# A fused attention and FFN kernel: statistics of the layer norms ahead of the FFN on VectorE, and the first four output groups of each expansion on token halves

## The chip, the cores and the metric

The kernel runs on one core of a Trainium2 chip. The metric is device time of one execution in microseconds (us); the number that counts is the median of several runs. The core has engines that work side by side, each through its own queue in order: TensorE (PE in the profile, its weight loads PEld), VectorE (DVE), ScalarE (ACT), GpSimd (POOL) and SyncE (SP), which here issues all large DMA transfers.

## What is computed

Two layers, each an attention block and a feed-forward block with residuals, on 2048 tokens of width 1024, in bfloat16:

```python
def _layernorm(x, axis=-1, eps=1e-5):
    m = jnp.mean(x, axis=axis, keepdims=True)
    v = jnp.var(x, axis=axis, keepdims=True)
    return (x - m) / jnp.sqrt(v + eps)
...
def _A_ref(x, wqkv, wo):     # 32 heads of 32; 8 keys per token, 2 tokens apart
    ...
    logits = jnp.einsum("bhsd,bhswd->bhsw", q, kg) * scale
    logits = jnp.where(mask[None, None, :, :], logits, -1e9)
    attn = _softmax(logits, axis=-1)
    o = jnp.einsum("bhsw,bhswd->bhsd", attn, vg)
    ...
def _B_ref(x, w1, b1, w2, b2):   # 1024 -> 3584 -> 1024
    h = jnp.einsum("bsd,df->bsf", x, w1) + b1
    r = jnp.where(h > zero, h, zero)
    h = r * r
    return jnp.einsum("bsf,fd->bsd", h, w2) + b2
...
x = x + _A_ref(_layernorm(x), A_wqkv, A_wo)
x = x + _B_ref(_layernorm(x), B_w1, B_b1, B_w2, B_b2)
x = x + _A_ref(_layernorm(x), A_wqkv, A_wo)
x = x + _B_ref(_layernorm(x), B_w1, B_b1, B_w2, B_b2)
```

## The kernel before

The tokens are cut into four blocks of 512 (even and odd tokens are kept apart, so that keys two tokens apart are neighbours). A layer and a block make a unit: units 0 to 3 are layer one, 4 to 7 layer two. A unit goes through six stages, each a Python generator:

- `gen_SA`: loads four tiles of 128 tokens, normalises each (`ln_transpose`) and transposes it by DMA into `xnT`, features on partitions. This is the attention norm.
- `gen_SQ` in two parts, `SQa` (K and Q) and `SQb` (V): L260 multiplies weights with `xnT`, ScalarE copies the result out of PSUM (L262).
- `gen_S2`: the windowed attention, on VectorE. L308 multiplies Q with shifted K, L327 adds the products in a tree, TensorE reduces over the head (L354, 16 small matmuls of 32 columns for each half of 256 tokens; L341 in unit 0), then softmax (L364 to L378), a DMA transpose of the probabilities (`pb`, L388), and the product with V (L401 to L404) into `oT`.
- `gen_SW`: the output projection (L447), residual `xm` (L449, VectorE), the FFN norm (`ln_transpose` of `xm` into a second `xnT`), and L453, which adds the bias b2 to `xm` once the norm has read it.
- `gen_SF`: the FFN, in two halves of the 3584 features (16 and 12 groups of 128). A group is a chain of eight L475 matmuls, 512 tokens wide, into the PSUM tile `ph`; ScalarE makes `r` (L479, bias and ReLU) and `r2t` (L480, square). L496 multiplies the squares of a half with w2.

`ln_transpose` has two ways to the statistics. With `dve_stats` two `bn_stats` (L171) and one `bn_aggr` (L173) on VectorE give mean and variance; ScalarE takes the logarithm and the exponential for the reciprocal root (L175, L176), and VectorE multiplies to `nmr` (L177). Without it ScalarE does all: a pass for the sum (L180), a scaling (L182), a pass for the squares (L184), logarithm, exponential and `nmr` (L186 to L188). Both passes are written into the tile `xn`. In both cases L189 on ScalarE writes the normalised tile to `xn` (two buffers) and L190 transposes it (SP queue, SyncE waits for `xn`, the DMA takes some us). Before the change VectorE takes the statistics in `gen_SA` of unit 0 and in `gen_SW` of unit 7, ScalarE in all others.

`build` writes the order of the program. The primary stages stand in the row SQa(0), SQb(0), then for each u: SQa(u+1), SW(u), SQb(u+1), SF(u). At each `yield` of a primary stage a position is counted up and `service` moves the side tasks (SA, S2) on by their launch and due positions: S2(u+1) runs beside SW(u), SQb(u+1) and SF(u), SA(u+2) beside SF(u). This written order is a priority for a scheduler, which places each engine's instructions by estimated readiness; what is under `high_priority` (L262, L449, L479, L480 and the sums of L502 to L511) goes first. The order on each engine is fixed when the program is built. Waits between engines are put in by the tile framework from reads and writes of tiles, for the part of a tile that is read.

PSUM has six tiles for `py`, `pq` and `ph` together (`ps_mm`) and two for the attention logits. Weights come in tiles of 1 MB through five buffers, issued by SP three ahead of use (`get_w`). `xnT` has two buffers, `xt` two.

Of the kernel before, what the change touches and what calls it, by code (L numbers as in the profile page):

```python
# [7 lines left out]
F32 = mybir.dt.float32  # L8
# [9 lines left out]
BLK = 512  # L18
# [8 lines left out]
class _Kernel:  # L27
# [403 lines left out]
    def gen_SW(self, u):  # L431
        nc = self.nc
        layer, b = divmod(u, self.NB)
        KD, KF, NCH, D, F = self.KD, self.KF, self.NCH, self.D, self.F
        st = self.state[u]
        oT = st.pop("oT")
        xnT = self.act.tile([128, KD, BLK], BF, name="xnT", tag="xnT")
        wos = [self.get_w(("wo", u, g)) for g in range(D // 512)]
        xbs = []
        for tl in range(4):  # L440
            t = b * 4 + tl
            xr = self.load_x_tile(layer, t, "xt")
            xm = self.xp.tile([128, D], F32, name="xm", tag="xm", bufs=4)
            for db in range(D // 512):
                py = self.ps_mm.tile([128, BLK], F32, name="py", tag="mm")
                for c in range(NCH):
                    nc.tensor.matmul(py[:], oT[:, c, tl * 128:(tl + 1) * 128], wos[db][:, c, :], start=(c == 0), stop=(c == NCH - 1))  # L447
                with self.tc.high_priority():
                    nc.vector.tensor_tensor(xm[:, db * 512:(db + 1) * 512], py[:], xr[:, db * 512:(db + 1) * 512], ALU.add)  # L449
                yield  # L450
            xbs.append(xm)
            self.ln_transpose(xm[:], xnT, tl, dve_stats=(u == self.n_layers * self.NB - 1), evac_act=(u == 0))
            nc.vector.tensor_tensor(xm[:], xm[:], self.b2b[:], ALU.add)  # L453
            yield
        st["xnT_B"] = xnT
        st["xbs"] = xbs

    def gen_SF(self, u):
        nc = self.nc
        layer, b = divmod(u, self.NB)  # L460
        KD, KF, NCH, D, F = self.KD, self.KF, self.NCH, self.D, self.F
        st = self.state[u]
        xnT = st.pop("xnT_B")
        xbs = st.pop("xbs")
        last_layer = (layer == self.n_layers - 1)
        NHALF = len(self.f_halves)
        for hf, (g0, g1) in enumerate(self.f_halves):
            r2 = []
            for g in range(g0, g1):
                wt = self.get_w(("w1", u, g))  # L470
                for cc in range(4):
                    f_idx = g * 4 + cc
                    ph = self.ps_mm.tile([128, BLK], F32, name="ph", tag="mm")
                    for kd in range(KD):
                        nc.tensor.matmul(ph[:], wt[:, kd, cc * 128:(cc + 1) * 128], xnT[:, kd, :], start=(kd == 0), stop=(kd == KD - 1))  # L475
                    r = self.small.tile([128, BLK], BF, name="r", tag="r", bufs=3)
                    r2t = self.r2p.tile([128, BLK], BF, name="r2t", tag="r2")
                    with self.tc.high_priority():
                        nc.scalar.activation(out=r[:], in_=ph[:], func=ACTF.Relu, bias=self.b1T[:, f_idx:f_idx + 1], scale=1.0)  # L479
                        nc.scalar.activation(out=r2t[:], in_=r[:], func=ACTF.Square)  # L480
                    r2.append(r2t)
                    yield
            final = (hf == NHALF - 1)
            KFH = 4 * (g1 - g0)
            for db in range(D // 512):
                w2s = [self.get_w(("w2", u, hf, db, gi)) for gi in range(len(self.w2_groups[hf]))]
                kmap = []
                for gi, (k0, k1) in enumerate(self.w2_groups[hf]):
                    for j in range(k1 - k0):
                        kmap.append((gi, j))  # L490
                for tl in range(4):
                    t = b * 4 + tl
                    py = self.ps_mm.tile([128, BLK], F32, name="py2", tag="mm")
                    for kf in range(KFH):
                        gi, j = kmap[kf]
                        nc.tensor.matmul(py[:], r2[kf][:, tl * 128:(tl + 1) * 128], w2s[gi][:, j, :], start=(kf == 0), stop=(kf == KFH - 1))  # L496
                        if kf % 7 == 6 and kf != KFH - 1:
                            yield
                    xbsl = xbs[tl][:, db * 512:(db + 1) * 512]
                    if not final:  # L500
                        with self.tc.high_priority():
                            nc.vector.tensor_tensor(xbsl, py[:], xbsl, ALU.add)  # L502
                    elif last_layer:
                        xo = self.small.tile([128, BLK], BF, name="xo", tag="xo", bufs=3)
                        with self.tc.high_priority():
                            nc.vector.tensor_tensor(xo[:], py[:], xbsl, ALU.add)  # L506
                        nc.sync.dma_start(self.par_tile(self.out_par, t)[:, db * 512:(db + 1) * 512], xo[:])
                    else:
                        xo = self.small.tile([128, BLK], F32, name="xof", tag="xof", bufs=2)
                        with self.tc.high_priority():  # L510
                            nc.vector.tensor_tensor(xo[:], py[:], xbsl, ALU.add)  # L511
                        nc.sync.dma_start(self.xs[layer][t * 128:(t + 1) * 128, db * 512:(db + 1) * 512], xo[:])
                    yield

        st["sf_done"] = True
# [15 lines left out]
    def build(self):  # L531
# [33 lines left out]
        def advance(t, upto):  # L565
            if t['gen'] is None:
                t['gen'] = gens[t['kind']](t['u'])
            while not t['finished'] and t['done'] < upto:
                try:
                    r = next(t['gen'])  # L570
                    if r == "BLOCK":
                        assert upto < t['n'] + 500, "blocked generator at forced completion"
                        break
                    t['done'] += 1
                except StopIteration:
                    t['finished'] = True

        def service(pos):
            for t in tasks:
                if t['finished'] or pos < t['launch']:  # L580
                    continue
                span = max(1, t['deadline'] - t['launch'])
                f = (pos - t['launch']) / (span * t['margin'])
                tgt = t['n'] + 1 if (f >= 1.0 or pos >= t['deadline']) else f * t['n']
                advance(t, tgt)

        pos = 0
        for i, (kind, u) in enumerate(prim):
            for t in tasks:
                if not t['finished'] and t['deadline'] <= cum[i]:  # L590
                    advance(t, t['n'] + 1000)
            g = gens[kind](u)
            for _ in g:
                pos += 1
                service(pos)
            pos = cum[i + 1]
            service(pos)
# [52 lines left out]
```

## Time and profile before

| what | value |
|---|---|
| median of 3 runs | 1322.74 us (1322.34 to 1323.29) |
| span of the profiled execution, first to last instruction | 1317.7 us |
| granted TensorE clock, mean | 0.988 |
| TensorE busy | 94% of the span |
| VectorE, ScalarE busy | 62%, 48% |
| DMA, mean | 189 GB/s |
| L475 matmuls, 128x512 (1792) | 383 ns each, by the record |
| L260 matmuls, 128x512 (1536) | 381 ns each, by the record |
| L479, L480 on ScalarE (224 each) | 682 ns, 627 ns |
| L180, L184, L189 on ScalarE, from `xm` (28, 28, 32) | 1054, 1148, 1241 ns |
| L308, L327 on VectorE (128, 98) | 1224, 1218 ns |
| transposes of `xn` (64), issue to landing | 3.5 us median |

The time of the profiled execution is given by its span alone; the runs' times hold start and end besides. Matmuls overlap, so a record is longer than the distance from one start to the next (0.216 us for 512 columns where nothing waits); on VectorE and ScalarE neighbours overlap by about 0.1 us in the records. Groups are told by line, engine, operation and names; after the bar stand busy time, mean of one, and the idle time before them with what ended it.

### The profile page before, as it was taken

The page shows a single profiled execution, that of the slowest core. Times are in us where ns is not written, and L with a number is a line of the kernel's source. Part 1 is how long each engine was busy: PE and PEld are TensorE (multiplying, and loading weights), DVE is VectorE, ACT ScalarE, POOL GpSimd, SP SyncE. Part 2 cuts the span into 40 slices and gives each one's busy share as a digit, 9 for nine tenths or more (in the row PEclk, how much of TensorE's full clock was granted, in tenths as well). Part 3 has the DMA queues.
Part 4 walks back from the last instruction along what each step waited for, and adds up shares of the span by engine and source line. Part 5 has one row for each costly group of instructions (what it writes and reads, how often), then busy time and mean ns, then how long its engine had stood idle before and what let it go on. Part 6 is the DMA issues. An engine that isn't in the chain of part 4 may idle for free.

```text
span 1317.7 us, 15544 instructions
## 1 busy us (share of the span) xinstructions
PE 1243.7 (94%) x6112; PEld 633.7 (48%) x6112; DVE 811.7 (62%) x1132; ACT 636.8 (48%) x1185; POOL 2.9 (0%) x9
## 2 busy tenths in 40 slices
PE   2998899998999999999999999999999999996998
PEld 1664444554445544465444654455544554442443
DVE  2569997197932969239781597617794199915011
ACT  3633854159342682427912396314944167142622
POOL 0000000000000000000000000000000000000000
PEclk9998899999999999999999999999999999998999
DMA  9573883668747695558955589455984578448341
GB/s 247 153 199 97 220 217 123 214 194 230 176 144 239 191 241 169 165 194 231 250 172 186 199 234 245 160 192 176 260 235 132 195 219 221 134 150 227 128 136 56
DMA packets 282218, 248.77 MB, mean 189 GB/s; under 512 B 109984, under 2 KB 245152, under 8 KB 282144
## 3 DMA queue, kind: packets, MB, share of 16 engines
q1 hardware_dynamic: 278544, 247.76, 64.0%
q0 software_dynamic: 3600, 0.01, 0.5%
q8 instruction: 48, 0.79, 0.2%
q14 instruction: 26, 0.21, 0.1%
HBM read 209.98 MB, written 12.58 MB: 169 GB/s over the span
## 4 chain that ended last, share of the span: by engine, by line
PE 63%; ACT 18%; DVE 9%; DMA 8%; issue 2%; SPq 0%; ACTq 0%; DVEq 0%
PE py L496 28%; PE ph L475 19%; PE pq L260 13%; DMA xnT<-xn 5%; DVE P L308 3%; ACT r L479 3%; ACT xn L180 3%; ACT xn L189 3%; ACT xn L184 3%; ACT r2t L480 3%; DVE P L327 2%; PE py L447 2%; DMA xt<-xs 1%; ACT vT L262 1%; DMA xt<-in_A_x_dram 1%
## 5 line engine op out<-in xcount | busy, mean ns | idle before, releaser
L475 PE MATMUL ph<-xnT,wt 128*128 128x512 bf16 x1792 | 396.7, 383 | 31.2 <-DMA xnT<-xn 17.4
L496 PE MATMUL py<-wt,r2t 128*128 128x512 bf16 x1792 | 391.4, 379 | 7.2 <-ACT r2t L480 7.1
L260 PE MATMUL pq<-xnT,wt 128*128 128x512 bf16 x1536 | 341.0, 381 | 25.8 <-DMA xnT<-xn 23.5
L475 PEld LDWEIGHTS <-wt 128*128 128x128 bf16 x1792 | 175.6, 99 | 247.0 <-issue 42.6
L260 PEld LDWEIGHTS <-wt 128*128 128x128 bf16 x1536 | 218.8, 144 | 136.5 <-issue 26.0
L496 PEld LDWEIGHTS <-r2t 128*128 128x128 bf16 x1792 | 175.0, 98 | 221.0 <-ACT r2t L480 11.9
L479 ACT ACTIVATE r<-ph,b1T 128x512 bf16<-128x512 f32 x224 | 152.7, 682 | 265.2 <-PE ph L475 265.0
L401 DVE TENSOR_TENSOR pr<-pb,vT 128x2048 bf16<-128x2048 bf16 x128 | 155.2, 1226 | 42.4 <-DMA pb<-p 42.4
L308 DVE TENSOR_TENSOR P<-qT,kT 128x2048 bf16<-128x2048 bf16 x128 | 153.7, 1224 | 44.7 <-ACT qT L262 44.7
L480 ACT ACTIVATE r2t<-r 128x512 bf16<-128x512 bf16 x224 | 138.1, 627 | 4.1
L262 ACT CAST kT<-pq 128x512 bf16<-128x512 f32 x64 | 37.4, 585 | 191.0 <-PE pq L260 191.0
L447 PE MATMUL py<-wt,oT 128*128 128x512 bf16 x512 | 115.2, 385 | 5.7 <-DVE oT L404 5.7
L327 DVE TENSOR_TENSOR P<-P 128x2048 bf16<-128x2048 bf16 x98 | 119.1, 1218 | 0.4
L506 DVE TENSOR_TENSOR xo<-py,xm 128x512 bf16<-128x512 f32 x32 | 22.1, 692 | 131.0 <-PE py L496 131.0
L511 DVE TENSOR_TENSOR xof<-py,xm 128x512 f32<-128x512 f32 x32 | 22.1, 692 | 113.8 <-PE py L496 99.2
L402 DVE TENSOR_TENSOR pr<-pr 128x1024 bf16<-128x1024 bf16 x128 | 87.3, 688 | 0.0
L447 PEld LDWEIGHTS <-oT 128*128 128x128 bf16 x512 | 50.4, 99 | 68.3 <-DVE oT L404 7.2
L502 DVE TENSOR_TENSOR xm<-py,xm 128x512 f32<-128x512 f32 x64 | 44.1, 690 | 54.9 <-PE py L496 54.9
L262 ACT CAST qT<-pq 128x512 bf16<-128x512 f32 x64 | 37.3, 583 | 66.5 <-PE pq L260 66.5
L271 DVE COPY khalo<-kT 128x56 bf16<-128x56 bf16 x8 | 1.4, 180 | 85.2 <-ACT kT L262 85.2
L403 DVE TENSOR_TENSOR pr<-pr 128x512 bf16<-128x512 bf16 x128 | 53.2, 421 | 0.0
L180 ACT ACTIVATE xn<-xm 128x1024 bf16<-128x1024 f32 x28 | 29.5, 1054 | 44.6 <-DVE xm L449 40.1
(54 smaller groups left out, 559.8 us busy)
## 6 DMA issues: line engine op xcount, KB each, us to landing
wt<-in_B_w_dram SPq DMA_DIRECT2D x88, 1024.0 KB, 6.3
wt<-in_A_wqkv_dram SPq DMA_DIRECT2D x48, 1024.0 KB, 6.0
wt<-in_B_w_dram SPq DMA_DIRECT2D x32, 768.0 KB, 4.3
wt<-in_A_wo_dram SPq DMA_DIRECT2D x16, 1024.0 KB, 6.1
xt<-xs SPq DMA_DIRECT2D x32, 512.0 KB, 4.0
xt<-in_A_x_dram SPq DMA_DIRECT2D x32, 256.0 KB, 3.4
xs<-xof SPq DMA_DIRECT2D x32, 256.0 KB, 3.3
out_dram<-xo SPq DMA_DIRECT2D x32, 128.0 KB, 1.9
```

Of the source, the lines that this page charges most:

```text
L180: nc.scalar.activation(out=xn[:], in_=xt, func=ACTF.Identity, accum_out=s1[:])
L260: nc.tensor.matmul(pq[:], fetch(nm)[kd // 4][:, kd % 4, c0:D:8], xnT[:, kd, :], start=(kd == 0), stop=(kd == KD - 1))
L262: nc.scalar.copy(dst[:, c0, off:off + BLK], pq[:])
L308: pi = nc.vector.tensor_tensor(P[:], qT[:, c, None, hb * HB:(hb + 1) * HB].to_broadcast([128, W, HB]), _win_ap(kT[:, c, :], HALO + hb * HB ...
L327: nc.vector.tensor_tensor(other[:], other[:], cur[:], ALU.add)
L401: nc.vector.tensor_tensor(pr[:], pb[:], vwin, ALU.mult)
L402: nc.vector.tensor_tensor(pr[:, 0:4, :], pr[:, 0:4, :], pr[:, 4:8, :], ALU.add)
L447: nc.tensor.matmul(py[:], oT[:, c, tl * 128:(tl + 1) * 128], wos[db][:, c, :], start=(c == 0), stop=(c == NCH - 1))
L475: nc.tensor.matmul(ph[:], wt[:, kd, cc * 128:(cc + 1) * 128], xnT[:, kd, :], start=(kd == 0), stop=(kd == KD - 1))
L479: nc.scalar.activation(out=r[:], in_=ph[:], func=ACTF.Relu, bias=self.b1T[:, f_idx:f_idx + 1], scale=1.0)
L480: nc.scalar.activation(out=r2t[:], in_=r[:], func=ACTF.Square)
L496: nc.tensor.matmul(py[:], r2[kf][:, tl * 128:(tl + 1) * 128], w2s[gi][:, j, :], start=(kf == 0), stop=(kf == KFH - 1))
```

## The change

Two things change. `gen_SW` asks for `dve_stats` in every unit, not in unit 7 alone, so in units 0 to 6 the statistics of the four tiles are taken by L171, L173 and L177 on VectorE and L175, L176 on ScalarE. And in `gen_SF` the first weight tile (g = 0, four groups of 128 features) is worked off in another order: four PSUM tiles `ph` are taken at once, the chains of all four run on tokens 0 to 255 (tiles 0 and 1 of the norm), then the chains of all four on tokens 256 to 511. The evacuations of the four groups follow after both halves. The two new yields "PART" let `service` run, but do not count a position.

```diff
-            self.ln_transpose(xm[:], xnT, tl, dve_stats=(u == self.n_layers * self.NB - 1), evac_act=(u == 0))
+            self.ln_transpose(xm[:], xnT, tl, dve_stats=True, evac_act=(u == 0))
...
+        HB = BLK // 2
         for hf, (g0, g1) in enumerate(self.f_halves):
             r2 = []
             for g in range(g0, g1):
                 wt = self.get_w(("w1", u, g))
+                phs = None
+                if g == 0:
+                    phs = [self.ps_mm.tile([128, BLK], F32, name="ph", tag="mm") for _ in range(4)]
+                    for th in range(2):
+                        for cc in range(4):
+                            for kd in range(KD):
+                                nc.tensor.matmul(phs[cc][:, th * HB:(th + 1) * HB], wt[:, kd, cc * 128:(cc + 1) * 128],
+                                                 xnT[:, kd, th * HB:(th + 1) * HB], start=(kd == 0), stop=(kd == KD - 1))
+                            if th == 0 and cc % 2 == 1:
+                                yield "PART"
                 for cc in range(4):
                     f_idx = g * 4 + cc
-                    ph = self.ps_mm.tile([128, BLK], F32, name="ph", tag="mm")
-                    for kd in range(KD):
-                        nc.tensor.matmul(ph[:], wt[:, kd, cc * 128:(cc + 1) * 128], xnT[:, kd, :], start=(kd == 0), stop=(kd == KD - 1))
+                    if phs is not None:
+                        ph = phs[cc]
+                    else:
+                        ph = self.ps_mm.tile([128, BLK], F32, name="ph", tag="mm")
+                        for kd in range(KD):
+                            nc.tensor.matmul(ph[:], wt[:, kd, cc * 128:(cc + 1) * 128], xnT[:, kd, :], start=(kd == 0), stop=(kd == KD - 1))
...
-            for _ in g:
-                pos += 1
+            for r in g:
+                if r != "PART":
+                    pos += 1
                 service(pos)
```

## The prediction

> **What bounds the kernel now.** I read the page first, then TensorE's timeline around each start of an FFN, then the chain of waits and the other engines there.
>
> ```profile
> span 1317.7 us, 15544 instructions
> PE 1243.7 (94%) x6112; PEld 633.7 (48%) x6112; DVE 811.7 (62%) x1132; ACT 636.8 (48%) x1185; POOL 2.9 (0%) x9
> L475 PE MATMUL ph<-xnT,wt 128*128 128x512 bf16 x1792 | 396.7, 383 | 31.2 <-DMA xnT<-xn 17.4
> L496 PE MATMUL py<-wt,r2t 128*128 128x512 bf16 x1792 | 391.4, 379 | 7.2 <-ACT r2t L480 7.1
> ```
> TensorE is the bound: 5632 matmuls of 512 columns start 0.216 us apart where nothing waits (64 L447 run from 1190.84 in 13.81 us), 1216 of 1317.7 us. Only its gaps can be won: 31.2 us before L475 (normalised rows that are not yet transposed) and 7.2 us before L496 (squares that ScalarE hasn't delivered). The timeline of unit 3, and of the two odd units:
>
> ```profile
> 623.87 10.30 PE L475 MATMUL ph<-xnT,wt 128*128 128x512 bf16 x47 [1.71 <-ACT nmean L182]
> 621.27 1.06 ACT L180 ACTIVATE xn<-xt 128x1024 bf16<-128x1024 f32 x1 [0.68 <-DMA xnT<-xn]
> 627.92 0.66 ACT L479 ACTIVATE r<-ph,b1T 128x512 bf16<-128x512 f32 x1
> 656.71 0.64 ACT L480 ACTIVATE r2t<-r 128x512 bf16<-128x512 bf16 x1
> 147.56 7.01 PE L475 MATMUL ph<-xnT,wt 128*128 128x512 bf16 x25 [6.36 <-DMA xnT<-xn]
> 131.09 2.48 DVE L449 TENSOR_TENSOR xm<-py,xt 128x512 f32<-128x512 f32 x4 [0.40 <-PE py L447]
> ```
> The chain of waits in the last unit:
>
> ```profile
> 1202.39 1.24 ACT xn L189
> 1203.65 6.79 DMA xnT<-xn
> 1210.53 1.25 ACT xn L189
> 1211.80 3.88 DMA xnT<-xn
> 1215.81 29.30 PE ph L475 x128
> ```
> Call E the end of a unit's last matmul before its FFN (622.0 in unit 3). TensorE then idles 6.5, 4.1, 2.6, 1.9, 1.7, 2.0, 2.5 and 11.2 us in units 0 to 7. But in units 1 to 5 the first half of the FFN ends with ScalarE: it has 16 L479/L480 pairs and the next block's four attention norms, and the 16th square is ready at E+37.1, 38.2, 35.4 (656.71+0.64), 35.1 and 34.1 us. TensorE alone needs E+31.3 (16 chains and one inserted reduction, 28.0, and 15 matmuls, 3.2). So a gap closed at the start is worth only what ScalarE's end moves.
>
> **What moves, by instruction.**
>
> ```profile
> L171 DVE BATCH_NORM_STATS2 stats<-xm 128x6 f32<-128x512 f32 x8 | 5.4, 690 | 0.1
> L173 DVE BATCH_NORM_AGGREGATE mv<-stats 128x2 f32<-128x12 f32 x8 | 1.6, 202 | 0.1
> L177 DVE SCALAR_TENSOR_TENSOR nmr<-mv,rstd 128x1 f32<-128x1 f32 x8 | 1.2, 154 | 1.5 <-ACT rstd L176 1.4
> ```
> 28 tiles (units 0 to 6) leave ScalarE without L180, L182, L184, their two accumulator reads and L188: 1054+187+200+1148+187+293 ns = 3.07 us a tile, 86 us in all. VectorE gains 2x690+202+154 = 1.74 us a tile, 49 us; started back to back (1.27 us for two L171) I count 0.62, 0.62, 0.13 and 0.12. VectorE serves its queue in order, so place decides, and the built program's order gives it.
>
> **Units 1 to 5, -11.9 us.** In the new order, walked with unit 3's times (L308, L327 and L453 start 1.14 us apart, L449 0.60), the four mean-times-rstd results come at 604.6, 609.2, 613.2 and 616.4; each L189 ends 1.3 us later and its transpose lands 3.1 to 7.4 us after (rows of this unit): tiles 0 and 1 by 614, tile 3 at 621 to 625. First half wanted at E, second at E+3.5: the gap goes. What then ends is ScalarE. It starts the next block's first L180 when tile 2's transpose frees its buffer, E-3.2 to E-1.5 instead of E-0.7; up to the first L479 it has 9.6 us of work (two whole attention norms and three casts), so E+6.4 to E+7.6 instead of E+5.9, but with more norm work behind it. From the first L479 to the 16th L480 it took 29.4 us; take off 1.2 of waiting for xt and 2.8 of norm steps now done earlier, add one L189 (1.14) that the order puts ahead of the last pair: 26.6. The end is E+33.0 to E+34.2, I take 33.6: gains of 3.5, 4.6, 1.8, 1.5 and 0.5 us. Bounds: E+31.3, TensorE's own, is -23.4; E+35.4, ScalarE no earlier than now, is -2.9 (units 1 and 2 gain 1.7 and 2.8, units 4 and 5 lose 0.3 and 1.3).
>
> VectorE's 6 us a unit I cost at nothing here: what covers them is the lead of the last L327 over the second reduction on TensorE (L354, nine chains into the FFN), 9.3 us in unit 3 (630.1 against 639.4). By the walk it ends at E+12.9 and TensorE comes at E+15.5. If that cover goes, TensorE stalls, and the first 2.3 us of that cost nothing, since ScalarE ends later anyway. SP's queue issues the same DMAs; it puts two xt loads ahead of the transposes of p, which frees ScalarE of a wait (4.6 us in the chain at 483.40).
>
> **Unit 0, +11.1 us.** Here VectorE is full, and the statistics stand behind attention work. L449 of tiles 2 and 3 cannot start before 131.09 (they wait for L447) and end at 133.5. Behind them, up to tile 3's L177: 8 L308, 7 L327 and 3 L453 at 1.14, six L171, four L173, four L177 and a copy: 25.3 us, so 158.8. L189 and a transpose (1.3+3.2): 163.3. Tile 1 lands at about 149, so the first half runs, then reduction one (its last L327 ends at 157.2), then TensorE waits for 163.3. The granted clock fell to 0.5 from 143.71 to 150.54 in the gap before (the span's 140 to 160 shows 0.83), so I count 4.3 us of half speed here, 2.1 lost: the four chains end at 168.9. Five chains and one matmul (8.9) lead to the second reduction at 177.7 (VectorE 177.2), 0.4 for it, 6.9 chains: 190.0 where it was 177.92. The 0.9 us that L496 then waited goes: +11.1. If TensorE keeps its clock +9; if VectorE or the transpose lags by 3 us, +14.
>
> The page "TensorE: Matmul & The Clock Gate" of the Trainium skill (section on the clock gate) says activity is judged over free-running windows of 3413 ns, and warns of gaps over about 3.4 us. Against the trace this is too mild: unit 2's gap of 2.6 us was followed by 0.5 until 467.98, while unit 6's 2.5 us was not. By its limit unit 0's two long gaps still throttle, and the sum stays.
>
> **Unit 6, +0.7.** No attention norm follows; tile 3 lands 0.3 us late, and the second reduction stands only 13 matmuls behind the halves (TensorE 1101.3, VectorE's last L327 1103.9): 2.9 us of waits for the 2.5 us gap, and up to 2 more if the clock falls.
>
> **Unit 7, -4.6.** Statistics are unchanged; only the halves act. Tile 1 landed at 1210.4 (1203.65+6.79), tile 3 at 1215.7. The first half's 3.45 us fits in between, at half clock at first, so the second starts at once and warm: four chains end at 1219.3 to 1219.9 instead of 1224.3. If the halves run cold throughout, -2.5.
>
> **The halves themselves, +1.0.** 64 matmuls of 256 for 32 of 512, and 32 more weight loads, in eight units. No row has 256 columns. Exactly half of 0.216 costs nothing; a straight line through 0.216 and the reductions of 32 columns (16 add 0.39 us, 24 ns each) gives 114 ns, 0.37 us a unit, 3.0 in all. I take 1.0, nearer the 512 row. Four of six PSUM buffers are held longer; the seventh chain needs one at E+10.4, and the first L479 ends by E+8.2.
>
> The same page (section on the back-to-back issue gap) gives two rules: N/2.4+2.5 ns, 109 ns here, an estimated 0.6 us in all; and a sustained 81 ns instead of 56 at N=128, because loads and matmuls share the spacing. If those 25 ns hold at 256, it speaks against the change: an estimated 13 us, and the sum would be +8. The reductions at 24 ns a pair argue for the first.
>
> **The sum.** +11.1 -11.9 +0.7 -4.6 +1.0 = -3.7 us on a span of 1317.7: 1314.0. The median of the runs, 1322.74, lies 5.0 us above that span, start and end, untouched: 1319.0.
>
> **Rivals.**
> *ScalarE's end does not move* (slower). Tile 2's transpose may land as late as the 7.35 us row of unit 3, so the next block's norms start no earlier. With the end at E+35.4 units 1 to 5 give 2.9, the sum is +5.3: 1328.0. It decides from E+34.3 on, where the sum crosses zero. For it: the next norm needs that same buffer; against: the vT casts no longer queue behind norms.
> *ScalarE gets ahead of TensorE*: E+31.3, -23.4, sum -15.2: 1307.5. For it: 3.07 us a tile less work; against: it mostly idles meanwhile, waiting for VectorE and buffers.
> *Weight loads show* at 256 columns: 24 ns for 256 more loads is 6.2 us, 1324.2; with L475's whole load of 99 ns, 25 us, 1343. Or the halves don't part: 4.6 lost in unit 7, 3.5 in unit 0, 1327.1. Against the latter: the built order gives each half its own DMA wait.
>
> **How the numbers follow.** Forecast 0.50, of it 0.28 below 1320.1, 0.19 within 0.2% (2.6 us, about what this kernel's timing can tell from no change), 0.03 above. ScalarE unmoved 0.25 (0.22 slower, 0.03 same). ScalarE ahead 0.15, faster. Loads or halves 0.10 (0.09 slower, 0.01 same). Faster 0.43, same 0.23, slower 0.34. The forecast's own range is 1314 to 1325 (unit 0 by -2 to +3, units 1 to 5 by the two ends of the walk); it goes up past ScalarE unmoved and down near ScalarE ahead: 1309 to 1330.
>
> **What would show it.** L475's wait for xnT gone in units 1 to 5, while L496's wait for r2t stays at about 2 us a unit; in unit 0 a wait of some 6 us in the middle of the 256-wide matmuls; in unit 7 the first of them near 1210 less the shift. Wrong, if L496 no longer waits in units 2 to 4, if L354 waits over 3 us, or if 256-wide matmuls start over 115 ns apart.

## The result, and the profile after

The changed kernel takes 1335.12 us (median of four runs, 1331.59 to 1338.5); the kernel before took 1322.54 us beside it (1321.28 to 1323.29). The ratio is 1.0098 (95% interval 1.0073 to 1.0123): 1% slower, clear of noise, where the forecast was 1319.0. Everything below is made on the one profiled execution of each kernel, whose span went from 1317.7 to 1330.3 us.

The page of the changed kernel, first the span, the engines and the granted clock by fortieths of the span, then three groups. L510 is the old L496 (squares times w2); the old L475 is now L478 (the token halves, 256 wide) and L489; L493 and L494 are the old L479 and L480.

```profile
span 1330.3 us, 15910 instructions
PE 1250.4 (94%) x6253; PEld 663.3 (50%) x6368; DVE 848.4 (64%) x1244; ACT 563.8 (42%) x1017; POOL 2.9 (0%) x9
...
PEclk9999799999999998999989999999989999999999
...
L510 PE MATMUL py<-wt,r2t 128*128 128x512 bf16 x1759 | 402.3, 387 | 19.5 <-ACT r2t L494 17.5
...
L489 PE MATMUL ph<-xnT,wt 128*128 128x512 bf16 x1497 | 333.0, 379 | 2.1
...
L478 PE MATMUL ph<-xnT,wt 128*128 128x256 bf16 x512 | 64.1, 291 | 18.7 <-DMA xnT<-xn 18.7
```

The idle time in front of the expansion fell from 31.2 to 20.8 us (18.7 + 2.1), as meant. But the idle time in front of the w2 matmuls rose from 7.2 to 19.5 us, and their mean went from 379 to 387 ns: some ran at a lower clock, as shown below. (1759 of the 1792 are in this record; a missing one looks like a gap of at most 0.05 us at full clock.) ScalarE has 73 us less work (636.8 to 563.8), VectorE 37 more; ScalarE's relief does not show in the time.

To see where, I cut each unit at E, the end of the last matmul before its FFN (its start plus 0.216 us), and measured to the start of the expansion's second half. "Gap" is E to the first expansion matmul; "w2 wait" sums the starts of w2 matmuls of the first half that lie over 0.45 us apart, less 0.216 each; "half clock" is the time at a granted clock of 0.5 in the stretch. From the two traces, us:

| unit | before: gap, w2 wait, half clock, total | after: gap, w2 wait, half clock, total | difference | predicted |
|---|---|---|---|---|
| 0 | 6.52, 0.93, 6.83, 65.45 | 9.06, 0, 17.07, 75.13 | +9.7 | +11.1 |
| 1 | 4.07, 0, 3.41, 61.50 | 0, 4.67, 3.41, 62.23 | +0.7 | -3.5 |
| 2 | 2.62, 2.80, 3.41, 62.60 | 0, 3.83, 6.83, 62.45 | -0.2 | -4.6 |
| 3 | 1.88, 2.22, 0, 59.81 | 0, 4.67, 6.83, 63.29 | +3.5 | -1.8 |
| 4 | 1.72, 2.10, 0, 59.49 | 0, 4.21, 3.41, 61.37 | +1.9 | -1.5 |
| 5 | 2.05, 0.85, 0, 58.56 | 0, 3.15, 6.83, 61.78 | +3.2 | -0.5 |
| 6 | 2.49, 0, 0, 58.14 | 0 (2.51 inside the expansion), 0, 0, 58.41 | +0.3 | +0.7 |
| 7 | 11.16, 0, 10.24, 67.92 | 4.85, 0, 6.83, 62.75 | -5.2 | -4.6 |

Unit 0's E itself came 1.3 us earlier, so its net loss in the span is 8.4. The sum, with that, is the 12.6 us of the span. Units 0, 6 and 7 came within 3 us of the forecast. Units 1 to 5 were to give 11.9 and cost 9.2.

Unit 3 shows it. Before the change its last two waits at L496 were these; the second line is from the chain of waits, and is all that was left of the half's w2 work:

```profile
656.03 0.39 PE L496 MATMUL py<-wt,r2t 128*128 128x512 bf16 x1 [0.89 <-ACT r2t L480]
657.40 24.56 PE py L496 x113
```

In the changed kernel, the timeline of TensorE, then of ScalarE, then of SP's queue (the DMAs that SyncE issues; E is 630.97):

```profile
630.97 7.15 PE L478 MATMUL ph<-xnT,wt 128*128 128x256 bf16 x64
637.95 8.80 PE L489 MATMUL ph<-xnT,wt 128*128 128x512 bf16 x39
...
659.07 3.28 PE L510 MATMUL py<-wt,r2t 128*128 128x512 bf16 x13
663.24 0.39 PE L510 MATMUL py<-wt,r2t 128*128 128x512 bf16 x1 [0.89 <-ACT r2t L494]
664.62 0.39 PE L510 MATMUL py<-wt,r2t 128*128 128x512 bf16 x1 [0.98 <-ACT r2t L494]
666.98 8.22 PE L510 MATMUL py<-wt,r2t 128*128 128x512 bf16 x24 [1.98 <-ACT r2t L494]
```

```profile
630.36 1.06 ACT L180 ACTIVATE xn<-xt 128x1024 bf16<-128x1024 f32 x1 [3.59 <-DMA xnT<-xn]
...
640.02 0.67 ACT L493 ACTIVATE r<-ph,b1T 128x512 bf16<-128x512 f32 x1
...
664.44 1.25 ACT L189 ACTIVATE xn<-xt,nmr,rstd 128x1024 bf16<-128x1024 f32 x1
665.57 0.69 ACT L493 ACTIVATE r<-ph,b1T 128x512 bf16<-128x512 f32 x1
666.30 0.63 ACT L494 ACTIVATE r2t<-r 128x512 bf16<-128x512 bf16 x1
```

```profile
620.41 0.54 SPq L150 DMA_DIRECT2D wt<-in_B_w_dram  x1
622.97 1.23 SPq L190 DMA_TRANSPOSE xnT<-xn  x1
624.30 1.04 SPq L200 DMA_DIRECT2D xt<-xs  x1
```

TensorE starts at E with nothing in its way. ScalarE idles 3.59 us, until tile 2's transpose, issued at 622.97, gives back an `xn` buffer at 630.36; then it does two whole attention norms of the next block, and takes the first expansion result at 640.02, E+9.05. Its 16th square is ready at 666.93, E+35.96; before it was E+35.36. TensorE waits three times in a row, the longest, 1.98 us, at the end; from there to the second half of the expansion (666.98 to 694.26) it takes 27.3 us, where it took 24.4 (657.40 to 681.81; the 24.56 of the chain counts to the end of the last record). The granted clock after that, in columns that give the busy time of TensorE, the clock, the DMA share and GB/s for each stretch:

```profile
662.60:666.00 3.40, 0.78 (x2) 1.00 1.00 182
666.00:669.40 3.40, 2.42 (x6) 0.50 0.96 281
669.40:672.80 3.40, 3.40 (x9) 0.50 1.13 309
672.80:676.20 3.40, 3.40 (x17) 1.00 0.20 77
```

After a stretch of 3.4 us in which TensorE worked 0.78, it ran at half speed for 6.8 us: nine matmuls in a stretch where 17 would fit.

### The profile page after: what moved, and what is told of

Its sections match the earlier page's. It is cut to its first block, busy times and chain, and to the rows that moved or that the text cites. A ratio compares the mean times of both kernels' runs of the same rounds, so it can differ in the third digit from the quotient of the medians.

```text
span 1330.3 us, 15910 instructions
## 1 busy us (share of the span) xinstructions
PE 1250.4 (94%) x6253; PEld 663.3 (50%) x6368; DVE 848.4 (64%) x1244; ACT 563.8 (42%) x1017; POOL 2.9 (0%) x9
## 4 chain that ended last, share of the span: by engine, by line
PE 65%; DVE 15%; ACT 12%; DMA 6%; issue 2%; SPq 0%; ACTq 0%; DVEq 0%
PE py L510 29%; PE ph L489 18%; PE pq L260 12%; DVE P L327 3%; DVE P L308 3%; ACT r L493 3%; PE py L447 3%; DMA xnT<-xn 2%; ACT r2t L494 2%; PE ph L478 2%; ACT xn L189 2%; DVE xm L449 1%; DVE pr L401 1%; ACT xn L184 1%; ACT xn L180 1%
## 5 line engine op out<-in xcount | busy, mean ns | idle before, releaser
L510 PE MATMUL py<-wt,r2t 128*128 128x512 bf16 x1759 | 402.3, 387 | 19.5 <-ACT r2t L494 17.5
L260 PE MATMUL pq<-xnT,wt 128*128 128x512 bf16 x1501 | 339.9, 382 | 28.6 <-DMA xnT<-xn 23.3
L489 PE MATMUL ph<-xnT,wt 128*128 128x512 bf16 x1497 | 333.0, 379 | 2.1
L510 PEld LDWEIGHTS <-r2t 128*128 128x128 bf16 x1792 | 177.7, 99 | 241.5 <-ACT r2t L494 24.0
L260 PEld LDWEIGHTS <-wt 128*128 128x128 bf16 x1536 | 218.9, 144 | 137.8 <-issue 26.6
L493 ACT ACTIVATE r<-ph,b1T 128x512 bf16<-128x512 f32 x224 | 152.4, 684 | 273.9 <-PE ph L489 264.8
L489 PEld LDWEIGHTS <-wt 128*128 128x128 bf16 x1536 | 149.7, 98 | 177.9
L494 ACT ACTIVATE r2t<-r 128x512 bf16<-128x512 bf16 x224 | 138.8, 630 | 4.5
L447 PE MATMUL py<-wt,oT 128*128 128x512 bf16 x504 | 112.4, 379 | 4.5 <-DVE oT L404 4.0
L478 PE MATMUL ph<-xnT,wt 128*128 128x256 bf16 x512 | 64.1, 291 | 18.7 <-DMA xnT<-xn 18.7
L478 PEld LDWEIGHTS <-wt 128*128 128x128 bf16 x512 | 53.2, 104 | 29.8 <-issue 14.5
L262 ACT CAST qT<-pq 128x512 bf16<-128x512 f32 x64 | 37.4, 584 | 66.6 <-PE pq L260 65.4
L175 ACT ACTIVATE lnv<-mv,eps 128x1 f32<-128x1 f32 x36 | 10.5, 293 | 118.1 <-DVE mv L173 118.1
```

The lines of the kernel that those rows point to most:

```text
L260: nc.tensor.matmul(pq[:], fetch(nm)[kd // 4][:, kd % 4, c0:D:8], xnT[:, kd, :], start=(kd == 0), stop=(kd == KD - 1))
L262: nc.scalar.copy(dst[:, c0, off:off + BLK], pq[:])
L478: nc.tensor.matmul(phs[cc][:, th * HB:(th + 1) * HB], wt[:, kd, cc * 128:(cc + 1) * 128], xnT[:, kd, th * HB:(th + 1) * HB], start=(kd == ...
```

## The experiments

Theory A: in units 1 to 5 the first FFN half ends with ScalarE, which puts the next block's attention norms among the squares. TensorE's earlier start buys no time, only a longer wait at L510, and the wait costs clock on top. Rival V: VectorE's added statistics are what costs. Further rivals stand in the expectations. Each kernel ran on one chip with the kernel before, whose medians there were 1320.05 (first four experiments), 1320.33 (next four) and 1321.44 us (last two). For comparison with the changed kernel I use its ratio or its profile by units; the table with all of them follows the experiments.

**1. The statistics alone.** The kernel before with `dve_stats=True` in `gen_SW`, no halves.

```diff
-            self.ln_transpose(xm[:], xnT, tl, dve_stats=(u == self.n_layers * self.NB - 1), evac_act=(u == 0))
+            self.ln_transpose(xm[:], xnT, tl, dve_stats=True, evac_act=(u == 0))
```

> The statistics of all FFN norms on VectorE, the expansion as before (all four groups 512 wide). Theory A (ScalarE's queue ends the first FFN half in units 1 to 5, whatever TensorE does at its start): units 1 to 5 as in the changed kernel, about +9 us against before; unit 0 must wait for tile 3 before any L475, about +12; unit 7 gains nothing: 1342 to 1348 us. Theory B (the halves cost, the statistics are free): within 3 us of before, 1322.

1334.79 us (1331.77 to 1337.71), ratio 1.0101 (1.0064 to 1.0139). Unit 0 got 13.5 us longer, with a gap of 20.96 us (one reduction of small matmuls lies in it) and 20.5 us of half clock. In units 1 to 5 the gaps fell from 12.3 to 5.1 us in sum, the w2 waits rose from 8.0 to 14.2, and the total stayed (302.0 to 302.3). A's size was too high: the loss is nearly all unit 0's (unit 6 adds 2.1). ScalarE's end is the same in both kernels, E+35.4 in the mean of units 1 to 5; what is missing here against the changed kernel is half clock (10.2 us for 27.3).

**2. The halves alone.** The kernel before with the token halves and "PART", and the statistics as they were.

```diff
+                phs = None
+                if g == 0:
+                    phs = [self.ps_mm.tile([128, BLK], F32, name="ph", tag="mm") for _ in range(4)]
...
```

> The four groups on token halves, statistics on ScalarE in units 0 to 6 as before. Theory A: the gap at the FFN start goes in units 1 to 6, but ScalarE ends as before, so units 1 to 5 give at most the clock they lose now and may lose some at the new wait; unit 7 gives 5 us, unit 0 about 3, unit 6 about 2.5: 1313 to 1320 us, and the wait of the w2 matmuls for the squares grows from 7 us to 15 or more. Theory V (VectorE's added 49 us is what holds the changed kernel back): units 1 to 5 give their 23 us as well, 1290 to 1295.

1325.27 us (1323.52 to 1328.89), ratio 1.0037 (1.0021 to 1.0054). All gaps in units 0 to 6 went, and yet units 1 to 5 took 14.0 us more: w2 waits from 8.0 to 24.6, half clock from 6.8 to 30.7. VectorE has no statistics here, so V falls for these units. A erred in the sign too: a wait that only moved would have cost nothing. The 14.0 us are 2.7 of later squares (E+36.5 in the mean, where it was 35.9) and 11.3 behind the 16th square, where TensorE has no gap but 23.3 us of half clock. The halves do save 2.6 us in unit 0, 2.4 in unit 6 and 4.0 in unit 7.

**3. Four buffers for `xn`.** The changed kernel, so that the next block's L180 need not wait for tile 2's transpose.

```diff
-        xn = self.xp.tile([128, D], BF, name="xn", tag="xn")
+        xn = self.xp.tile([128, D], BF, name="xn", tag="xn", bufs=4)
```

> The changed kernel with four buffers for xn in place of two. Theory C (the late transpose of tile 2 holds the buffer that the next attention norm needs, so ScalarE starts at E-0.6 as before): its first L180 moves to E-4 or earlier, the 16th square comes some 3.5 us sooner in each of units 1 to 5 and the half clock after the wait mostly goes: 1311 to 1320 us. Theory O (the order on ScalarE, two whole attention norms ahead of the first L493, sets it, not the start): under 5 us gained, 1328 to 1335.

1322.19 us (1319.18 to 1324.58), ratio 1.001 (0.9993 to 1.0026): between the two expectations. The first attention L180 of units 1 to 5 now starts 1.7 to 4.2 us earlier, but the 16th square only 0.6 to 1.3 us (mean E+34.4 in place of 35.4). Units 1 to 5 gain 7.6 us, since the w2 waits fall to 15.6 and half clock to 20.5; another 4.6 lies ahead of unit 0's E (135.14 in place of 139.75). So the buffer is a part of the cause, not the whole.

**4. The attention norm held back.** The changed kernel; the first L180 of each attention norm is put behind the 16th square of the FFN half on ScalarE. Both are on one engine, so this fixes an order and adds no wait.

```diff
-            nc.scalar.activation(out=xn[:], in_=xt, func=ACTF.Identity, accum_out=s1[:])
+            fi = nc.scalar.activation(out=xn[:], in_=xt, func=ACTF.Identity, accum_out=s1[:])
+            if after is not None:
+                self.tc.add_manual_dep(fi.ins, after.name,
+                                       mybir.DependencyInfo(mybir.DependencyClass.NoSync, mybir.DependencyReason.DATA),
+                                       reason="attention norm after the squares of the first FFN half")
...
-            self.ln_transpose(xt, xnT, tl, dve_stats=(u == 0), evac_act=(1 <= u <= 2))
+            self.ln_transpose(xt, xnT, tl, dve_stats=(u == 0), evac_act=(1 <= u <= 2),
+                              after=(self.state[u - 2]["sq16"] if u >= 2 else None))
...
-                        nc.scalar.activation(out=r2t[:], in_=r[:], func=ACTF.Square)
+                        qi = nc.scalar.activation(out=r2t[:], in_=r[:], func=ACTF.Square)
+                    if hf == 0:
+                        st["sq16"] = qi.ins
```

> The changed kernel, with the next block's attention norms held behind the 16th square on ScalarE. Theory A: no wait for squares is left, the first FFN half with its w2 part takes TensorE's own 55.7 us in units 1 to 5 (311 us together now, 279 then): 1300 to 1306 us. Theory V (VectorE's load): no change beyond 3 us.

1305.66 us (1302.8 to 1308.94), ratio 0.9882 (0.9845 to 0.9919). Its group of w2 matmuls (L517 there):

```profile
L517 PE MATMUL py<-wt,r2t 128*128 128x512 bf16 x1792 | 390.3, 379 | 2.3 <-ACT r2t L499 2.3
```

The idle time in front of them is 2.3 us in place of 19.5, the mean is 379 ns again. The 16th square is ready at E+31.8 to E+32.2, and each of units 1 to 5 takes 56.2 to 56.7 us. VectorE's statistics are all still there: A holds, V falls for the second time.

**5. Unit 0's statistics back on ScalarE.** The changed kernel with one argument changed.

```diff
-            self.ln_transpose(xm[:], xnT, tl, dve_stats=True, evac_act=(u == 0))
+            self.ln_transpose(xm[:], xnT, tl, dve_stats=(u > 0), evac_act=(u == 0))
```

> The changed kernel with unit 0's FFN norms computed on ScalarE again; units 1 to 6 keep VectorE's statistics, the halves stay. Theory A (unit 0 loses because its statistics stand behind attention work on VectorE): unit 0's time from the end of the projection to the second half of the FFN goes back from 75.1 us to about 62.8, as with the halves alone, while the attention before it gets 1 to 2.5 us longer: about 10 us less than the changed kernel, 1322 to 1328. Rival U (unit 0's loss comes from the halves there, which leave TensorE two gaps in place of one): no gain, 1333 to 1337.

1322.07 us (1317.97 to 1329.96), ratio 1.0016 (0.9995 to 1.0036). Unit 0 takes 64.1 us in place of 75.1; units 1 to 5 stay (311.4 against 311.1). The loss in unit 0 is the statistics'.

**6. The halves with the norm held back.** Experiment 2 with the order of experiment 4; FFN statistics as before the change.

> The halves, statistics as in the kernel before, and the first L180 of the next block's attention norm held behind the 16th square of the first FFN half. Theory A (the L496 wait of units 1 to 5 comes from attention norms that ScalarE puts among the squares): each of units 1 to 5 falls from 61 to 66 us with the halves alone to about 56.5, some 34 us in all: 1288 to 1296. Rival N (with FFN statistics on ScalarE too, the held-back norms come too late for the next unit's projections, which then wait): part of it is given back ahead of E, 1297 to 1306 or above.

1285.22 us (1282.04 to 1286.32), ratio 0.9729 (0.9711 to 0.9747), below what A expected. ScalarE in its unit 3 (E is 605.96; L498 and L499 are the ReLU and the square):

```profile
612.60 0.67 ACT L498 ACTIVATE r<-ph,b1T 128x512 bf16<-128x512 f32 x1
...
632.54 0.69 ACT L498 ACTIVATE r<-ph,b1T 128x512 bf16<-128x512 f32 x1 [0.38 <-PE ph L494]
633.26 0.63 ACT L499 ACTIVATE r2t<-r 128x512 bf16<-128x512 bf16 x1
634.27 0.69 ACT L498 ACTIVATE r<-ph,b1T 128x512 bf16<-128x512 f32 x1 [0.38 <-PE ph L494]
634.99 0.63 ACT L499 ACTIVATE r2t<-r 128x512 bf16<-128x512 bf16 x1
635.52 1.04 ACT L180 ACTIVATE xn<-xt 128x1024 bf16<-128x1024 f32 x1
```

ScalarE now waits for TensorE (0.38 us for each of the last results) and not the other way round; the norm starts when the last square is done, and the next projections do not miss it (idle time in front of their matmuls 25.2 us in all, before the change 25.8), so N falls. The same halves that cost 5 us in experiment 2 are worth 22 us here (against experiment 7).

**7. The kernel before with the norm held back**, neither statistics nor halves.

> The kernel before, with only the next block's first L180 held behind the 16th square. Theory A: the L496 waits of units 2 to 5 (8 us) and of unit 0 (0.9 us) go, the start gaps of 1.7 to 4.1 us stay: 1311 to 1316. Rival S (in the kernel before the late squares come from the late start, not from the norms): the waits stay and the time stays within 3 us, 1319 to 1325.

1307.28 us (1306.29 to 1310.59), ratio 0.9908 (0.9888 to 0.9929), lower than either expected. All w2 waits are gone, S falls. Of the start gaps 10.4 of 12.3 us stayed; more than the waits was won because unit 1's gap of 4.07 us is 1.62 now and half clock in units 1 to 5 halved (6.8 to 3.4).

**8. The statistics ahead in VectorE's queue.** Experiment 4 with L171, L173, L175 to L177 under `high_priority`.

```diff
+            with self.tc.high_priority():
+                for sg in range(nsg):
+                    nc.vector.bn_stats(out=stats[:, sg, :], in_=xr[:, sg, :])
+                nc.vector.bn_aggr(out=mv[:], in_=stats[:])
...
```

> The changed kernel with the first L180 held behind the 16th square (1305.7 us) and, further, the statistics of the FFN norms ahead of the attention work on VectorE. Theory A (unit 0's loss is VectorE's queue place alone, not VectorE's load): unit 0's time from the end of the projection to the second half falls from 74.9 us to 62 to 67, units 1 to 5 stay at 56 to 57: 1294 to 1300. Rival L (VectorE is full there: what is put ahead pushes the attention rows back, and the projection or the reductions wait instead): 1303 to 1309.

1299.13 us (1297.23 to 1301.06), ratio 0.9838 (0.9822 to 0.9855). The four statistics of unit 0's tiles 2 and 3 on VectorE's timeline, first in the changed kernel, then here (L171 is L174 there):

```profile
143.40 0.69 DVE L171 BATCH_NORM_STATS2 stats<-xm 128x6 f32<-128x512 f32 x1
...
146.26 0.69 DVE L171 BATCH_NORM_STATS2 stats<-xm 128x6 f32<-128x512 f32 x1
...
149.28 0.69 DVE L171 BATCH_NORM_STATS2 stats<-xm 128x6 f32<-128x512 f32 x1
...
153.27 0.69 DVE L171 BATCH_NORM_STATS2 stats<-xm 128x6 f32<-128x512 f32 x1
```

```profile
133.46 0.68 DVE L174 BATCH_NORM_STATS2 stats<-xm 128x6 f32<-128x512 f32 x1
...
134.65 1.87 DVE L174 BATCH_NORM_STATS2 stats<-xm 128x6 f32<-128x512 f32 x3
```

They come right behind the residual sums, 10 to 17 us earlier, and unit 0 falls from 74.9 to 62.7 us. VectorE's work is the same; it is the place in the queues that costs (ScalarE's two small steps of the statistics, L175 and L176, were put ahead along with VectorE's). Part is given back: units 1 to 6 got 3.4 us longer.

**9. More work for TensorE.** The changed kernel, with 20 further w2 matmuls ahead of the first w2 chain in units 1 to 5.

```diff
-                    py = self.ps_mm.tile([128, BLK], F32, name="py2", tag="mm")
+                    py = self.ps_mm.tile([128, BLK], F32, name="py2", tag="mm"); [nc.tensor.matmul(py[:], r2[0][:, 0:128], w2s[0][:, 0, :], start=True, stop=True) for _ in range(20 if hf == 0 and db == 0 and tl == 0 and 1 <= u <= 5 else 0)]
```

> The changed kernel with 20 matmuls added ahead of the first w2 chain in units 1 to 5 (the first L510 of the half, 20 times more, each starting the sum anew, so nothing is changed in the result): 4.3 us of work for TensorE in the place where it would wait for the last squares; ScalarE's order stays as it is. Theory A with the clock as its second half (ScalarE's end sets the first half, and the lump of waits costs half clock on top): the 100 added matmuls (21.6 us of work) cost nothing and the half clock of units 1 to 5 (27 us, 13.7 us lost) mostly goes: 1321 to 1329. Rival W (the granted clock falls for a reason other than these waits): the work only takes the place of the waits, 1332 to 1338. Rival B (TensorE itself is the bound in these stretches): up to 21.6 us more, 1350 or above.

1325.99 us (1322.09 to 1327.08), ratio 1.003 (1.0015 to 1.0045; the changed kernel's is 1.0098). With 21.6 us more work on TensorE the kernel is some 9 us faster. ScalarE's instructions stand in the same order and its 16th square is no earlier (E+35.1 to 37.4, against 34.4 to 36.1). In its unit 3 (E is 627.00; L507 are the added matmuls):

```profile
655.10 4.48 PE L507 MATMUL py<-wt,r2t 128*128 128x512 bf16 x20
659.42 3.40 PE L510 MATMUL py<-wt,r2t 128*128 128x512 bf16 x15
```

```profile
655.00:658.40 3.40, 3.40 (x18) 1.00 0.11 25
658.40:661.80 3.40, 3.40 (x18) 1.00 1.02 194
661.80:665.20 3.40, 1.79 (x9) 1.00 0.99 272
```

TensorE still waits 1.77 us for the last square here, but the clock stays at 1.00. Over units 1 to 5 half clock fell from 27.3 us to nothing and their time from 311.1 to 302.2. So the waits' clock was worth 9 us even though the squares came 0.4 us a unit later, and W and B fall.

**10. The best of them with four `xn` buffers**: experiments 6 and 3 together.

> The halves with the attention norm held back (1285.2 us), and four xn buffers. Theory A: the squares no longer bind there, so the buffers are worth nothing in units 1 to 5; what after_xn4 got ahead of unit 0's FFN (E at 135.1 in place of 139.8) may come back: 1279 to 1285. Rival X (the transposes still wait for xn in units 0 and 7): down to 1275.

1280.13 us (1279.33 to 1281.07), ratio 0.9693 (0.9678 to 0.9707), the fastest measured. Unit 0's E is at 135.95, 3.6 us earlier than in experiment 6; units 1 to 5 change by 1.1 us.

All of them by units, from their profiled executions, us:

| kernel | unit 0 | units 1-5: gaps | w2 waits | half clock | total |
|---|---|---|---|---|---|
| before | 65.5 | 12.3 | 8.0 | 6.8 | 302.0 |
| after | 75.1 | 0 | 20.5 | 27.3 | 311.1 |
| 1 statistics alone | 78.9 | 5.1 | 14.2 | 10.2 | 302.3 |
| 2 halves alone | 62.8 | 0 | 24.6 | 30.7 | 316.0 |
| 3 after, four `xn` | 75.6 | 0 | 15.6 | 20.5 | 303.6 |
| 4 after, norm held back | 74.9 | 0 | 3.1 | 0 | 282.1 |
| 5 after, unit 0 on ScalarE | 64.1 | 0 | 21.6 | 27.3 | 311.4 |
| 6 halves, norm held back | 63.0 | 0 | 1.5 | 0 | 280.2 |
| 7 before, norm held back | 64.9 | 10.4 | 0 | 3.4 | 290.3 |
| 8 experiment 4, statistics ahead | 62.7 | 0 | 6.0 | 0 | 285.0 |
| 9 after, 100 more matmuls | 75.6 | 0 | 1.8 | 0 | 302.2 |
| 10 experiment 6, four `xn` | 62.1 | 0 | 0.3 | 0 | 279.1 |

## Why the prediction was wrong

The step that failed is the one on units 1 to 5: "The end is E+33.0 to E+34.2, I take 33.6: gains of 3.5, 4.6, 1.8, 1.5 and 0.5 us." Its first half was right: the gaps went in all five units, and ScalarE ended the half in all five. Two things in it were wrong.

*ScalarE's end.* The 16th square was ready at E+36.1, 35.1, 36.0, 35.5 and 34.4, 35.4 in the mean: 1.8 us a unit later than 33.6, 9.1 in all. The mean is that of the rival "ScalarE's end does not move" (E+35.4; that it fits to the tenth is luck), with its mechanism in part: in unit 3 the 7.35 us row was the right one for tile 2's transpose (7.39, from 622.97 to 630.36), and the next norm waited for that buffer. I had the row before me and took a smaller one. The next norms began at E-1.4, E-0.6 and E-1.0 in units 2 to 4, but at E-3.1 and E-2.1 in units 1 and 5, within the forecast, and the squares came late there too. Two terms of the sum were too small: the first ReLU came at E+7.2 to E+9.1, not at E+6.4 to E+7.6, 1.1 us late in the mean; from there to the 16th square took 26.8 to 28.9 us for the 26.6 walked, 0.7 in the mean. Experiment 3 shows that the buffer explains 1.0 us of the end, experiment 4 that the norms among the squares explain 3.4 (E+35.4 to E+32.0).

*The clock.* The rival's time was 1328.0, and the kernel is slower still. I had priced the fall of the granted clock in unit 0 and let it stand as a risk in unit 6, but counted the wait at L496 as plain time; "the first 2.3 us of that cost nothing" is the same oversight. A wait at the start of a unit and the same wait at L496 are not one price: in unit 3, 1.88 and 2.22 us lay in two places before, and 4.67 us lie in one now. From the 16th square to the second half of the expansion TensorE took 24.5 us in each of units 1 to 5 before, at full clock throughout; in the changed kernel it took 25.9 to 27.3, 11.7 us more in sum, with no gap but 24.1 us at half clock. Experiment 9 takes 11.0 of the 11.7 away; its squares come 2.1 us later in sum, which leaves its gain of 9.0. Of the 21.1 us by which units 1 to 5 were off, 9.1 are thus ScalarE's end and 11.7 the clock behind it, which the sum put at nothing (the 0.3 left is rounding in the five gains).

The sum's last term was misread, without effect on the difference: of the 5.0 us put down to start and end, every run on record shows 1.7 or 1.8 (1332.05 for a span of 1330.3); the rest is that the profiled execution was faster than the median, after the change too.

The other steps held. Unit 0, +11.1 forecast, +8.4 measured: tile 1 was to land at about 149 and the expansion began at 148.81; in the middle the second half of the tokens was to start at 163.3 and did at 160.83, after a wait of 5.12 us; the w2 matmuls began at 187.26 for 190.0. That the loss is the statistics' is shown by experiment 5, that it is their queue place and not the load by 8. Unit 6, +0.7: a wait of 2.51 us at L354, +0.3. Unit 7, -4.6: -5.2. Units 0 and 6 in TensorE's timeline, unit 0 above, unit 6 below:

```profile
148.81 6.17 PE L478 MATMUL ph<-xnT,wt 128*128 128x256 bf16 x32 [8.90 <-DMA xnT<-xn]
...
160.83 5.31 PE L478 MATMUL ph<-xnT,wt 128*128 128x256 bf16 x32 [5.12 <-DMA xnT<-xn]
...
1121.27 0.57 PE L354 MATMUL lg<-ind,P 128*128 128x32 bf16 x16 [2.51 <-DVE P L327]
```

The halves themselves, +1.0: 64 matmuls took 6.98 us in unit 3 (637.95 less 630.97), 109 ns each, for the 6.91 of 32 matmuls of 512. They cost 0.07 us a unit, and the rivals on weight loads fall; the isolated rule of the Trainium skill ("TensorE: Matmul & The Clock Gate", section on the back-to-back issue gap), an estimated 109 ns, agrees; its sustained 131 ns for 512 columns does not (0.216 us here).

Of the signs named beforehand one spoke: L496's wait was to stay "at about 2 us a unit"; it went from 8.0 to 20.5 us over units 1 to 5. None of the three signs of being wrong appeared: L496 waited in units 2 to 4, L354 waited 2.51 us at most, the 256-wide matmuls started 109 ns apart. They watched the waits, and not the clock.

## What to carry to other kernels

When two waits sit in series behind one late engine, closing the first only lengthened the second here: order the late engine's own queue first (here the next block's norm behind the squares, 13 us by itself), and then the closed gap pays (22 us more, where alone it cost 5). Price a wait of TensorE by where it lies: short waits that are spread over several stretches of 3.4 us may be free of a clock loss that the same time in one stretch brings. An instruction that is moved to a less busy engine still has a place in that engine's queue, and in unit 0 that place, not its duration, was what it cost.

## What the runs showed of the hardware

All changes of the granted clock in a profile lie on one raster of 3.413 us. I cut the twelve profiles (both kernels and the ten experiments, from 25 us after the start) by that raster and took, for each stretch at full clock with 0.3 us or more of TensorE idle by the matmul records, what the next one was granted:

| idle in the stretch of 3.413 us | stretches | followed by clock 0.5 |
|---|---|---|
| 0.3 to 1.7 us | 99 | 0 |
| 1.7 to 2.0 us | 22 | 10 |
| over 2.0 us | 66 | 66 |

So in these profiles the sum of idle time in one stretch decides, and the limit is a little over half of it (1.8 to 2.0 of 3.413 us); it need not be one gap. In the changed kernel's unit 3 it was 2.6 us (3.40 less 0.78), in three pieces around two matmuls, none over 1 us within the stretch (the third is the first half of the wait of 1.98 us). The Trainium skill's page named above (section on the clock gate) has the window of 3413 ns, which these runs confirm, but warns only of gaps of about a whole one; the measurement is stricter. It also explains what puzzled me before the change, that a gap of 2.6 us in unit 2 cost clock and one of 2.5 us in unit 6 did not: by the same cut the first left 2.15 us in one stretch, the second was split in two of 1.2 and 1.1 us.

Why E of unit 0 lay anywhere from 135 to 143 us stays open. The two kernels with four `xn` buffers start their first matmul at 20.5 us, the others at 23.0 to 25.7; the kernels also differ ahead of that E in who takes the statistics of unit 0's first FFN tiles, and where.
